# Attention's two heads of a pair in two corners of TensorE's array, with one copy each for queries and x

## The chip, the cores and the metric

The kernel runs on one core of one Trainium2 chip. A core has five engines with queues of their own: TensorE (PE; its weight loads are shown apart, as PEld), VectorE (DVE), ScalarE (ACT), GpSimd (POOL) and SyncE (SP), which issues most of the DMAs. Products are made by TensorE into PSUM; the other engines work on SBUF and PSUM. The metric is the device time of one execution in microseconds, as the median of several. Before the change it is 1930.49 us (three runs, 1930.45 to 1933.51).

## What is computed

Three stages follow each other, all on 2304 tokens of 512 numbers. The change lies in the first.

```python
scores = scale * np.matmul(q, k.transpose(0, 1, 3, 2))   # 4 batches, 8 heads, 576 positions, 64 numbers
mask = (rel >= 0) & (rel < window)                       # window = 64
attn = np.exp(scores - np.max(scores)) / sum
x = attn @ v                                             # 2304 x 512

P = exp(x @ w_gate), normed over rows and columns 8 times
x = sum over 8 experts of P[:, e] * (relu(x @ w1[e]) @ w2[e])

out = one expert per token, chosen greedily up to a capacity, relu(x @ w1[e]) @ w2[e]
```

A position sees only itself and the 63 before it. So a block of 64 queries needs 128 keys: its own block and the one ahead of it.

## The kernel before

**Tiles of attention.** The 2304 positions make 18 tiles of 128 (NT). A tile holds two blocks of 64 queries (b = 0, 1) and eight heads, taken as four pairs (HP = 4). After a transpose the 128 partitions hold the two heads of a pair, 64 numbers each.

**Queries** (function attn, lines 533 to 546). Four transposes put a tile's queries into a PSUM tile of pool psb. Then ScalarE copies them into qbd, once for each head of the pair (line 541), into a matrix that is zero elsewhere: rows 0 to 63 of head 0 beside columns 0 to 63, rows 64 to 127 of head 1 beside columns 64 to 127. So one product over 128 rows gives both heads' scores and does not mix them. The zeros are written once at the start, on GpSimd.

**Keys** (keys_of). They are transposed in the same way and copied by VectorE into a ring of six tiles, kring (line 580).

**Scores** (scores). Per block and pair one product of 128 rows, 128 weight columns (qbd) and 128 keys. For b = 1 both key blocks lie in one tile (line 591); for b = 0 they lie in two, which one product reads with a stride (line 597); in each sixth tile, where the ring wraps, it takes two products of 64 keys (line 600). VectorE adds the mask and takes the maximum (line 605), ScalarE exponentiates (line 612).

**Values** (values). Line 621 transposes the probabilities, ScalarE copies them to pTs (line 626, in the space of hh and hl). Line 632 multiplies: 128 keys as rows, the values of both heads as 128 weight columns, the probabilities of both heads as 128 moving columns. Of the four quarters of the result two are used, head 0 with head 0 and head 1 with head 1. So x leaves PSUM in two parts of 64 partitions: each is rounded to fp16 by ScalarE into xh (line 643), and VectorE stores the rest into xl (line 645).

**What else runs.** Expert 0 of the second stage is worked at the same time: its first layer at line 773, its second at line 943, its weights' splitting at lines 345 and 347. Router logits follow each tile of x (lines 683 and 685). The value maximum of each tile is spread over the partitions by a transpose with one column (line 266) and a product with one row (line 271). From expert 1 on the first layer is line 865.

**What sets the order.** A planner (class Flow) puts all of this in one order, while the program is built. Every step is a generator that asks for an engine with a cost in microseconds (Rq: PE 0.88 for a score step, ACT 0.53 for a copy of queries); the planner keeps a time for each engine, honours what a step depends on and the buffers of the pools (psb has four), and takes the task of lowest rank among those that can start within 0.12. Attention's tiles have ranks from 20 on, expert 0's products 50: those fill TensorE when attention has nothing ready. The costs are part of the text, so another cost means another order on all engines.

Of the kernel before, what the change touches and what calls it, by code (L numbers as in the profile page):

```python
# [8 lines left out]
F32 = mybir.dt.float32  # L9
F16 = mybir.dt.float16  # L10
I32 = mybir.dt.int32
AF = mybir.ActivationFunctionType
OP = mybir.AluOpType
# [159 lines left out]
def body(ctx, tc, q, k, v, wg1, w11, w12, wg2, w21, w22, out):  # L173
    nc = tc.nc
    V, A, PE, G, SP = nc.vector, nc.scalar, nc.tensor, nc.gpsimd, nc.sync
# [8 lines left out]
    HP = H // 2  # L184
# [8 lines left out]
    pss = ExitStack()  # L193
    ps1 = ctx.enter_context(tc.tile_pool(name="ps1", bufs=2, space=PSUM))
    ps2 = ctx.enter_context(tc.tile_pool(name="ps2", bufs=2, space=PSUM))
    psb = pss.enter_context(tc.tile_pool(name="psb", bufs=4, space=PSUM))
# [9 lines left out]
    xh = base.tile([128, DC, N], F16, name="xh")  # L206
    xl = base.tile([128, DC, N], F16, name="xl")
# [21 lines left out]
    abase = att.enter_context(tc.tile_pool(name="abase", bufs=1))  # L229
# [245 lines left out]

    qbd = []
    for i in range(2):
        t = abase.tile([128, 2, HP, 128], F32, name=f"qbd{i}")
        G.memset(t, 0.0)
        qbd.append(t)  # L480
    pTs = [t.rearrange("p a b -> p (a b)")[:, o:o + 1024].bitcast(F32).rearrange("p (h k) -> p h k", h=HP)
           for o in (0, 1024) for t in hbuf[1]]
    ldqk, ldv, ldvs = {}, {}, {}
# [1 line left out]
    KR = 6  # L485
    KT = HP * 128
    kring = abase.tile([128, (KR + 1) * KT], F32, name="kring")

    def kslot(i):
        o = (KR - 1 - i % KR) * KT  # L490
        return kring[:, o:o + KT].rearrange("p (h b q) -> p h b q", h=HP, b=2)
# [16 lines left out]
    def load_v(i):  # L508
        ldv[i] = apool.tile([128, H, D], F32, name="ldv", bufs=3)
        rows(ldv[i], v, i * 128, 128)  # L510
        fl.at["v", i] = fl.load(256)
# [17 lines left out]
    def attn(i):  # L529
        r = 20 + i if i else 0.5  # L530
        fl.add(keys_of(i), r)
        a = yield Rq("PE", 0.45, [("q", i), ("go", i - 2) if i > 1 else None], "psb")
        pq = psb.tile([128, HP, 128], F32, name="pb")
        t = ldqk.pop(("q", i)).rearrange("p h d -> p (h d)")
        for hp in range(HP):
            PE.transpose(pq[:, hp], t[:, hp * 128:(hp + 1) * 128], ident)
        qb = qbd[i % 2]
        for h2 in range(2):
            c = yield Rq("ACT", 0.53, [a.end])
            s = slice(h2 * 64, h2 * 64 + 64)  # L540
            A.activation(qb[s, :, :, s].rearrange("p b h q -> p h b q"),
                         pq[s].rearrange("p h (b q) -> p h b q", b=2), AF.Copy)
        fl.release("psb", a.idx, c.end)
        first = yield Rq("DVE", 0.01, [c.end, ("kT", i)], "pn")
        pn = apool.tile([128, 2, HP, 128], F32, name="pn")
        mx = small.tile([128, 8], F32, name="mx")
        nm = small.tile([128, 8], F32, name="nm")
        sm = small.tile([128, 8], F32, name="sm")
        for b in range(2):
            fl.add(scores(i, b, pn, mx, nm, sm), r)  # L550

        y = yield Rq("DVE", 0.5, [("ex", i, 0), ("ex", i, 1), ("vm", i), ("vm", max(i - 1, 0))])
        V.tensor_scalar(xinv[:, i:i + 1], vmax[:, i:i + 1], vmax[:, max(i - 1, 0):max(i - 1, 0) + 1], 1e-30,
                        op0=OP.max, op1=OP.max)
        V.tensor_scalar(sm, sm, 1e-9, xinv[:, i:i + 1], op0=OP.add, op1=OP.mult)
        rs = small.tile([128, 8], F32, name="rs")
        V.reciprocal(rs, sm)
        rc["pnleft", i] = 2
        for b in range(2):
            x = yield Rq("DVE", 0.66, [y.end])  # L560
            V.tensor_tensor(pn[:, b], pn[:, b], rs[:, b * HP:(b + 1) * HP, None].to_broadcast([128, HP, 128]), OP.mult)
            fl.add(values(i, b, pn, first.idx, x.end), r)

    def keys_of(i):
        b = yield Rq("PE", 0.45, [("k", i), ("go", i - 2) if i > 1 else None], "psb")
        pk = psb.tile([128, HP, 128], F32, name="pb")
        t = ldqk.pop(("k", i)).rearrange("p h d -> p (h d)")
        for hp in range(HP):
            PE.transpose(pk[:, hp], t[:, hp * 128:(hp + 1) * 128], ident)
        if i + 2 < NT:  # L570
            load_qk(i + 2)
        if i == 0:
            load_v(2)
            start_load(w2src(0), w2raw, 4, "w2r")
            SP.dma_start(wg2s, wg2.rearrange("(c p) e -> p c e", p=128))
            fl.at["wg2s"] = fl.load(16) + 8.0
        d = yield Rq("DVE", 0.66, [b.end])
        if i == 0:
            G.memset(kslot(-1)[:, :, 1], 0.0)
        V.tensor_copy(kslot(i), pk.rearrange("p h (b q) -> p h b q", b=2))  # L580
        fl.release("psb", b.idx, d.end)
        fl.at["kT", i] = d.end
        fl.add(largest_v(i), 5 + i)

    def scores(i, b, pn, mx, nm, sm):
        qb, kT = qbd[i % 2], kslot(i)
        f = yield Rq("PE", 0.88, [], "psb")
        pss = psb.tile([128, HP, 128], F32, name="pb")
        for hp in range(HP):
            if b:  # L590
                PE.matmul(pss[:, hp], qb[:, b, hp], kT[:, hp], start=True, stop=True)
            else:
                if i % KR:
                    o = (KR - 1 - i % KR) * KT + hp * 128
                    w = KT + 64
                    kk = kring[:, o:o + 2 * w].rearrange("p (b q) -> p b q", b=2)[:, :, 0:64]
                    PE.matmul(pss[:, hp].rearrange("p (b q) -> p b q", b=2), qb[:, b, hp], kk, start=True, stop=True)
                    continue
                for x, kk in enumerate((kT[:, hp, 0], kslot(i - 1)[:, hp, 1])):
                    PE.matmul(pss[:, hp, x * 64:x * 64 + 64], qb[:, b, hp], kk, start=True, stop=True)  # L600
        g = yield Rq("DVE", 1.0, [f.end])
        mk = masks[:, 2 * b + (1 if (2 * i + b) % NBLK == 0 else 0)]
        for hp in range(HP):
            u = b * HP + hp
            V.tensor_tensor_reduce(pn[:, b, hp], pss[:, hp], mk, 1.0, -3.0e38, OP.add, OP.max, mx[:, u:u + 1])  # L605
        us = slice(b * HP, b * HP + HP)
        V.tensor_scalar(nm[:, us], mx[:, us], -0.125, None, op0=OP.mult)
        fl.release("psb", f.idx, g.end)
        x = yield Rq("ACT", 1.55, [g.end])
        for hp in range(HP):  # L610
            u = b * HP + hp
            A.activation(pn[:, b, hp], pn[:, b, hp], AF.Exp, bias=nm[:, u:u + 1], scale=0.125, accum_out=sm[:, u:u + 1])
        fl.at["ex", i, b] = x.end
        if b:
            fl.at["go", i] = x.start

    def values(i, b, pn, held, dep):
        m = yield Rq("PE", 0.45, [dep], "psb")
        pp = psb.tile([128, HP, 128], F32, name="pb")
        for hp in range(HP):  # L620
            PE.transpose(pp[:, hp], pn[:, b, hp], ident)
        rc["pnleft", i] -= 1
        if not rc["pnleft", i]:
            fl.release("pn", held, m.end)
        n = yield Rq("ACT", 0.6, [m.end, ("av", 2 * i + b - 4) if i > 1 else None])
        A.activation(pTs[(2 * i + b) % 4], pp, AF.Copy, scale=8.0)
        fl.release("psb", m.idx, n.end)
        o = yield Rq("PE", 0.9, [n.end, ("vs", i)], "psb")
        vt = (ldvs[i], ldv[i])[b].rearrange("p h d -> p (h d)")
        px = psb.tile([128, HP, 128], F32, name="pb")  # L630
        for hp in range(HP):
            PE.matmul(px[:, hp], vt[:, hp * 128:(hp + 1) * 128], pTs[(2 * i + b) % 4][:, hp], start=True, stop=True)  # L632
        fl.at["av", 2 * i + b] = o.end
        if ("av", 2 * i + 1 - b) in fl.at:
            if i + 3 < NT:
                load_v(i + 3)
            if i + 2 < NT:
                load_vs(i + 2)
        c0 = i * 128 + b * 64
        for h2 in range(2):  # L640
            s = slice(h2 * 64, h2 * 64 + 64)
            x = yield Rq("ACT", 0.34, [o.end])
            A.activation(xh[s, :, c0:c0 + 64], px[s, :, s], AF.Copy)
            y = yield Rq("DVE", 0.4, [x.end])
            V.tensor_tensor(xl[s, :, c0:c0 + 64], px[s, :, s], xh[s, :, c0:c0 + 64], OP.subtract)  # L645
        fl.release("psb", o.idx, y.end)
        fl.at["xp", i, b] = y.end
        if ("xp", i, 1 - b) in fl.at:
            bg.done.add(("x", i))
            fl.at["x", i] = max(y.end, fl.at["xp", i, 1 - b])  # L650
# [739 lines left out]
    for e in range(1, E):  # L1390
        jobs += [(1, e), (0, e)]
        for _ in range(M2PLAN.get(e, len(m2left))):
            m, x = m2left.pop(0)
# [197 lines left out]
```

## Time and profile before

| | |
|---|---|
| median of three runs | 1930.49 us |
| profiled execution | 1943.79 us, span 1942.0 us |
| TensorE busy | 1859.8 us (96%) |
| VectorE busy | 1261.4 us (65%) |
| ScalarE busy | 916.1 us (47%) |
| mean granted clock of TensorE | 0.988 |

The profiled execution is some 13 us longer than the median; durations are read from it and compared with its own time. Products are pipelined: the next starts before the last has ended, so the pace of a burst is read from start to start and not from the mean duration. Attention ends at about 236 us, and the change concerns nothing behind it. A step at TensorE costs time at once if TensorE has work waiting; a step on another engine costs time only where TensorE waits for it.

### The profile page before, as it was taken

How to read it: one execution, taken by the hardware profiler on the slowest of the kernel's cores; microseconds unless marked ns; L12 is line 12 of the kernel's file. 1: busy time of each engine (PE TensorE's matmuls, PEld its weight loads, DVE VectorE, ACT ScalarE, POOL GpSimd, SP SyncE). 2: the span in 40 equal slices, each digit the busy share in tenths (PEclk: the TensorE clock that was granted, in tenths of full speed). 3: DMA queues.
4: the chain of work that ended last, by engine and by line, in shares of the span. 5: the costliest groups of instructions: out<-in, count | busy, mean ns of one | idle time of the engine just before them, and what ended most of it. 6: DMA issues, size and time to landing. Idle time of an engine off the chain costs nothing.

```text
span 1942.0 us, 39658 instructions
## 1 busy us (share of the span) xinstructions
PE 1859.8 (96%) x15605; PEld 1339.3 (69%) x15605; DVE 1261.4 (65%) x3845; ACT 916.1 (47%) x2493; POOL 110.8 (6%) x142
## 2 busy tenths in 40 slices
PE   6899999999999999999999999999999997899987
PEld 5777755776686766767766867677686773676765
DVE  7877796464666676676667666766747777465540
ACT  6777634552455555554554555455534442222222
POOL 0000000000000000000000000000000113223231
PEclk9999999999999999999999999999999998899999
DMA  8465301140134323323442434234231101435451
GB/s 188 89 131 120 83 1 44 59 160 1 55 120 143 119 93 118 138 88 116 145 136 83 131 117 145 93 99 157 88 104 28 43 20 64 175 123 172 159 211 29
DMA packets 172795, 203.32 MB, mean 105 GB/s; under 512 B 83000, under 2 KB 130104, under 8 KB 168512
## 3 DMA queue, kind: packets, MB, share of 16 engines
q1 hardware_dynamic: 164928, 157.78, 27.4%
q0 software_dynamic: 7680, 43.02, 6.3%
q8 instruction: 122, 2.00, 0.4%
q14 instruction: 65, 0.53, 0.1%
HBM read 143.05 MB, written 57.71 MB: 103 GB/s over the span
## 4 chain that ended last, share of the span: by engine, by line
PE 71%; DVE 11%; issue 6%; DMA 5%; ACT 4%; POOL 2%; SPq 0%; POOLq 0%; ACTq 0%; DVEq 0%
PE p L943 28%; PE p L865 17%; PE pb L865 12%; PE p L1302 4%; PE p L773 3%; DMA w2scr<-st2k 2%; DVE st2k L347 1%; DMA raw<-xrows,idx 1%; PE pb L1152 1%; DVE xl L645 1%; PE p L1314 1%; DMA raw<-in_moe_w_dram 1%; DMA ws<-st2k 1%; PE pb L632 1%; DVE pn L605 1%
## 5 line engine op out<-in xcount | busy, mean ns | idle before, releaser
L943 PE MATMUL p<-w2b,hh 128*128 128x512 f16 x2304 | 686.0, 379 | 0.0
L943 PE MATMUL p<-w2b,hl 128*128 128x512 f16 x1152 | 436.6, 379 | 0.0
L943 PEld LDWEIGHTS <-hh 128*128 128x128 f16 x2304 | 222.1, 99 | 218.2 <-issue 0.2
L865 PEld LDWEIGHTS <-w1b 128*128 128x128 f16 x4032 | 340.3, 98 | 22.2 <-issue 4.0
L865 PEld LDWEIGHTS <-w1x 128*128 128x128 f16 x3024 | 256.3, 98 | 21.1 <-issue 7.4
L865 PE MATMUL p<-th,w1x 128*128 128x192 f16 x1344 | 221.2, 246 | 4.3 <-ACT sa L877 2.2
L865 PE MATMUL pb<-xh,w1b 128*128 128x192 f16 x1344 | 221.3, 246 | 0.0
L943 PEld LDWEIGHTS <-hl 128*128 128x128 f16 x1152 | 112.6, 98 | 135.5 <-issue 0.6
L865 PE MATMUL pb<-xl,w1b 128*128 128x192 f16 x672 | 165.3, 246 | 0.0
L865 PE MATMUL p<-tl,w1x 128*128 128x192 f16 x672 | 165.3, 246 | 0.0
L347 DVE SCALAR_TENSOR_TENSOR st2k<-raw,wsc,st2k 128x512 f16<-128x512 f32 x128 | 91.9, 748 | 51.8 <-ACT st2k L345 51.5
L345 ACT ACTIVATE st2k<-raw,wsc 128x512 f16<-128x512 f32 x128 | 86.5, 713 | 71.3 <-DMA ws<-st2k 58.8
L959 DVE SCALAR_TENSOR_TENSOR acc<-p,SE,acc 128x512 f32<-128x512 f32 x126 | 94.0, 746 | 38.2 <-PE p L943 37.8
L1008 POOL TENSOR_TENSOR st2k<-tmp,st2k 128x512 f16<-128x512 f32 x18 | 24.7, 1370 | 1592.2 <-ACT tmp L1006 1571.1
L746 ACT ACTIVATE hh<-sb 128x192 f16<-128x192 f32 x168 | 61.0, 363 | 111.8 <-DVE sb L909 111.8
L865 PE MATMUL p<-th,w1b 128*128 128x192 f16 x672 | 110.6, 246 | 2.9 <-ACT sc L898 2.9
L746 ACT ACTIVATE hh<-sa 128x192 f16<-128x192 f32 x168 | 60.9, 363 | 107.2 <-DVE sa L883 107.2
L865 PE MATMUL pb<-xh,w1x 128*128 128x192 f16 x672 | 110.6, 246 | 0.0
L865 PE MATMUL p<-xh,w1b 128*128 128x192 f16 x672 | 110.6, 246 | 0.0
L883 DVE TENSOR_TENSOR sa<-pb,sa 128x192 f32<-128x192 f32 x168 | 60.0, 357 | 75.1 <-PE pb L865 72.6
L747 DVE SCALAR_TENSOR_TENSOR hl<-sa,hh 128x192 f16<-128x192 f32 x168 | 60.3, 359 | 72.1 <-ACT hh L746 72.1
L747 DVE SCALAR_TENSOR_TENSOR hl<-sb,hh 128x192 f16<-128x192 f32 x168 | 60.3, 359 | 71.7 <-ACT hh L746 71.7
(309 smaller groups left out, 3381.3 us busy)
## 6 DMA issues: line engine op xcount, KB each, us to landing
raw<-in_moe_w_dram SPq DMA_DIRECT2D x128, 512.0 KB, 5.6
ws<-st2k SPq DMA_DIRECT2D x128, 256.0 KB, 4.5
w2b<-w2scr SPq DMA_DIRECT2D x28, 512.0 KB, 7.1
w2scr<-st2k SPq DMA_DIRECT2D x48, 256.0 KB, 4.5
xrows<-st2k SPq DMA_DIRECT2D x18, 257.0 KB, 3.3
vs<-in_v_dram SPq DMA_DIRECT2D x35, 128.0 KB, 4.1
ldq<-in_q_dram SPq DMA_DIRECT2D x16, 256.0 KB, 4.6
ldk<-in_k_dram SPq DMA_DIRECT2D x16, 256.0 KB, 4.8
```

Source lines behind the costliest of these rows:

```text
L345: A.activation(hi, src, AF.Copy, scale=sc)
L347: V.scalar_tensor_tensor(lo, src, sc, hi, op0=OP.mult, op1=OP.subtract)
L605: V.tensor_tensor_reduce(pn[:, b, hp], pss[:, hp], mk, 1.0, -3.0e38, OP.add, OP.max, mx[:, u:u + 1])
L746: A.activation(hh[:, f, cols], src, AF.Relu)
L747: V.scalar_tensor_tensor(hl[:, f, cols], src, 0.0, hh[:, f, cols], op0=OP.max, op1=OP.subtract)
L773: PE.matmul(p[:, 0:w], w1v[wi][:, c, fs], x[:, c, ts], start=(n == 0), stop=(n == 3 * DC - 1))
L865: PE.matmul(bank[:, 0:HB], aq[wi][:, c, fs], xq[xi][:, c], start=(start and n == 0), stop=(n == 5), skip_group_check=True)
L883: V.tensor_tensor(t, b3[:, 0:HB], t, OP.add)
L943: PE.matmul(p, h[:, f, js], w2v[wi][:, f], start=(n == 0), stop=(n == 3 * FC - 1))
L959: V.scalar_tensor_tensor(acc[:, i], p, SE[:, e, i:i + 1], acc[:, i], op0=OP.mult, op1=OP.add)
L1008: G.tensor_tensor(xr[:, DM:2 * DM], xs, xr[:, 0:DM], OP.subtract)
L1302: PE.matmul(p[:, 0:CAP], wv1[f // 4][w][:, c, fs], xt[:, x * DC + c], start=(n == 0), stop=(n == 3 * DC - 1))
```

## The change

Queries are copied once, all 128 partitions, into a dense tile qT without zeros. The scores of the two heads of a pair become two products: head 0 with rows 0 to 63 and outputs 0 to 63, head 1 with rows 64 to 127 and outputs 64 to 127, so in two opposite corners of the array. The values become two products per pair as well: 64 weight columns and 64 moving columns each, head 0 to outputs 0 to 63, head 1 to outputs 64 to 127. The result is dense on 128 partitions, and x is copied once per block instead of twice. The planner's costs of the copies are set anew; those of the products stay.

```diff
--- before.py
+++ after.py
@@ -475,9 +475,7 @@
 
     qbd = []
     for i in range(2):
-        t = abase.tile([128, 2, HP, 128], F32, name=f"qbd{i}")
-        G.memset(t, 0.0)
-        qbd.append(t)
+        qbd.append(abase.tile([128, HP, 128], F32, name=f"qT{i}"))
     pTs = [t.rearrange("p a b -> p (a b)")[:, o:o + 1024].bitcast(F32).rearrange("p (h k) -> p h k", h=HP)
            for o in (0, 1024) for t in hbuf[1]]
     ldqk, ldv, ldvs = {}, {}, {}
@@ -534,12 +532,8 @@
         t = ldqk.pop(("q", i)).rearrange("p h d -> p (h d)")
         for hp in range(HP):
             PE.transpose(pq[:, hp], t[:, hp * 128:(hp + 1) * 128], ident)
-        qb = qbd[i % 2]
-        for h2 in range(2):
-            c = yield Rq("ACT", 0.53, [a.end])
-            s = slice(h2 * 64, h2 * 64 + 64)
-            A.activation(qb[s, :, :, s].rearrange("p b h q -> p h b q"),
-                         pq[s].rearrange("p h (b q) -> p h b q", b=2), AF.Copy)
+        c = yield Rq("ACT", 0.61, [a.end])
+        A.activation(qbd[i % 2], pq, AF.Copy)
         fl.release("psb", a.idx, c.end)
         first = yield Rq("DVE", 0.01, [c.end, ("kT", i)], "pn")
         pn = apool.tile([128, 2, HP, 128], F32, name="pn")
@@ -586,18 +580,20 @@
         qb, kT = qbd[i % 2], kslot(i)
         f = yield Rq("PE", 0.88, [], "psb")
         pss = psb.tile([128, HP, 128], F32, name="pb")
+
         for hp in range(HP):
-            if b:
-                PE.matmul(pss[:, hp], qb[:, b, hp], kT[:, hp], start=True, stop=True)
-            else:
-                if i % KR:
-                    o = (KR - 1 - i % KR) * KT + hp * 128
+            for s in (slice(0, 64), slice(64, 128)):
+                qs, o = qb[s, hp, b * 64:b * 64 + 64], pss[s, hp]
+                if b:
+                    PE.matmul(o, qs, kT[s, hp].rearrange("p b q -> p (b q)"), start=True, stop=True)
+                elif i % KR:
+                    c = (KR - 1 - i % KR) * KT + hp * 128
                     w = KT + 64
-                    kk = kring[:, o:o + 2 * w].rearrange("p (b q) -> p b q", b=2)[:, :, 0:64]
-                    PE.matmul(pss[:, hp].rearrange("p (b q) -> p b q", b=2), qb[:, b, hp], kk, start=True, stop=True)
-                    continue
-                for x, kk in enumerate((kT[:, hp, 0], kslot(i - 1)[:, hp, 1])):
-                    PE.matmul(pss[:, hp, x * 64:x * 64 + 64], qb[:, b, hp], kk, start=True, stop=True)
+                    kk = kring[s, c:c + 2 * w].rearrange("p (b q) -> p b q", b=2)[:, :, 0:64]
+                    PE.matmul(o.rearrange("p (b q) -> p b q", b=2), qs, kk, start=True, stop=True)
+                else:
+                    for x, kk in enumerate((kT[s, hp, 0], kslot(i - 1)[s, hp, 1])):
+                        PE.matmul(o[:, x * 64:x * 64 + 64], qs, kk, start=True, stop=True)
         g = yield Rq("DVE", 1.0, [f.end])
         mk = masks[:, 2 * b + (1 if (2 * i + b) % NBLK == 0 else 0)]
         for hp in range(HP):
@@ -627,9 +623,12 @@
         fl.release("psb", m.idx, n.end)
         o = yield Rq("PE", 0.9, [n.end, ("vs", i)], "psb")
         vt = (ldvs[i], ldv[i])[b].rearrange("p h d -> p (h d)")
-        px = psb.tile([128, HP, 128], F32, name="pb")
+        px = psb.tile([128, HP, 128], F32, name="pb")[:, :, 0:64]
         for hp in range(HP):
-            PE.matmul(px[:, hp], vt[:, hp * 128:(hp + 1) * 128], pTs[(2 * i + b) % 4][:, hp], start=True, stop=True)
+            for h2 in range(2):
+                s = slice(h2 * 64, h2 * 64 + 64)
+                PE.matmul(px[s, hp], vt[:, hp * 128 + h2 * 64:hp * 128 + h2 * 64 + 64], pTs[(2 * i + b) % 4][:, hp, s],
+                          start=True, stop=True)
         fl.at["av", 2 * i + b] = o.end
         if ("av", 2 * i + 1 - b) in fl.at:
             if i + 3 < NT:
@@ -637,12 +636,10 @@
             if i + 2 < NT:
                 load_vs(i + 2)
         c0 = i * 128 + b * 64
-        for h2 in range(2):
-            s = slice(h2 * 64, h2 * 64 + 64)
-            x = yield Rq("ACT", 0.34, [o.end])
-            A.activation(xh[s, :, c0:c0 + 64], px[s, :, s], AF.Copy)
-            y = yield Rq("DVE", 0.4, [x.end])
-            V.tensor_tensor(xl[s, :, c0:c0 + 64], px[s, :, s], xh[s, :, c0:c0 + 64], OP.subtract)
+        x = yield Rq("ACT", 0.36, [o.end])
+        A.activation(xh[:, :, c0:c0 + 64], px, AF.Copy)
+        y = yield Rq("DVE", 0.42, [x.end])
+        V.tensor_tensor(xl[:, :, c0:c0 + 64], px, xh[:, :, c0:c0 + 64], OP.subtract)
         fl.release("psb", o.idx, y.end)
         fl.at["xp", i, b] = y.end
         if ("xp", i, 1 - b) in fl.at:
```

TensorE, in the middle of attention: a run of value products followed by the scores of a tile and the transposes of the next tile's queries and keys. Each row gives the line, the result from its moving operand and weights, and weight columns by moving columns as the program writes them. Before:

```order
L632 MATMUL pb<-hh_81,vs 128x128 x4
L271 MATMUL pb<-mxr,ones 128x1
L621 MATMUL pb<-ident,pn 128x128 x12
L632 MATMUL pb<-hl_82,ldv 128x128 x4
L632 MATMUL pb<-hh_81,vs 128x128 x4
L632 MATMUL pb<-hl_82,ldv 128x128 x4
L597 MATMUL pb<-kring,qbd_128 128x128 x4
L591 MATMUL pb<-kring,qbd_128 128x128 x4
L536 MATMUL pb<-ident,ldq 128x128 x4
L569 MATMUL pb<-ident,ldk 128x128 x4
```

Now, in the corresponding place of the changed program:

```order
L617 MATMUL pb<-ident,pn 128x128 x12
L630 MATMUL pb<-hl_82,ldv 64x64 x8
L630 MATMUL pb<-hh_81,vs 64x64 x8
L630 MATMUL pb<-hl_82,ldv 64x64 x8
L596 MATMUL pb<-kring,qT_126 64x64 x16
L588 MATMUL pb<-kring,qT_126 64x128 x8
L534 MATMUL pb<-ident,ldq 128x128 x4
L563 MATMUL pb<-ident,ldk 128x128 x4
```

Each value step has eight products of 64x64 in the place of four of 128x128, each score step eight or sixteen. The shape changes three times here, from 128x128 to the half columns, to the corners and back.

ScalarE, in the first third of attention: the copies of probabilities (hh, hl), of x (xh) and the exponentials (pn). Before:

```order
L626 ACTIVATE hh_81<-pb 128x512
L626 ACTIVATE hl_82<-pb 128x512
L643 ACTIVATE xh<-pb 64x4x64 x2
L612 ACTIVATE pn,sm<-pn,nm 128x128 x4
L643 ACTIVATE xh<-pb 64x4x64 x2
L612 ACTIVATE pn,sm<-pn,nm 128x128 x12
```

Now:

```order
L622 ACTIVATE hh_81<-pb 128x512
L622 ACTIVATE hl_82<-pb 128x512
L640 ACTIVATE xh<-pb 128x4x64
L608 ACTIVATE pn,sm<-pn,nm 128x128 x4
L640 ACTIVATE xh<-pb 128x4x64
L608 ACTIVATE pn,sm<-pn,nm 128x128 x8
```

The copies of x stand as one row of 128 partitions where two of 64 stood.

TensorE, at the last value product of the last tile, with expert 0's first layer (p) and the router's products (wgs) beside it. Before:

```order
L773 LDWEIGHTS w1b
L773 MATMUL p_3002<-xl,w1b 128x384
L773 LDWEIGHTS w1b
L773 MATMUL p_3002<-xh,w1b 128x384
L632 MATMUL pb<-hl_82,ldv 128x128 x4
L683 LDWEIGHTS xh
L683 MATMUL pb<-wgs,xh 128x16
```

Now:

```order
L682 LDWEIGHTS xl
L682 MATMUL pb<-wgs,xl 128x8
L682 LDWEIGHTS xl
L682 MATMUL pb<-wgs,xl 128x8
L630 MATMUL pb<-hh_81,vs 64x64 x8
L630 MATMUL pb<-hl_82,ldv 64x64 x8
L680 LDWEIGHTS xh
L680 MATMUL pb<-wgs,xh 128x16
```

The last value product follows directly on the other one of its tile and on router products. By this place 384 products of line 773 (line 770 now) and 114 of line 943 (now 940) have been issued, where it was 480 and 144: attention is planned to end earlier among them.

## Rows read from the trace of the kernel before

**Rows 1.** The page, busy time of each engine with its share of the span.
```profile
PE 1859.8 (96%) x15605; PEld 1339.3 (69%) x15605; DVE 1261.4 (65%) x3845; ACT 916.1 (47%) x2493; POOL 110.8 (6%) x142
```

**Rows 2.** Stages: length, busy us of PE, PEld, DVE, ACT, POOL, clock, DMA.
```profile
0.00:50.00 50.00, 33.71 (x248) 29.54 (x249) 37.63 (x148) 31.64 (x88) 3.06 (x9) 0.93 0.80 183
50.00:100.00 50.00, 44.70 (x463) 38.84 (x462) 40.26 (x161) 37.45 (x128) 0.00 (x0) 1.00 0.45 86
100.00:240.00 140.00, 134.59 (x1036) 101.31 (x1034) 107.11 (x426) 98.78 (x317) 0.00 (x0) 1.00 0.53 116
240.00:300.00 60.00, 58.88 (x317) 31.36 (x316) 55.80 (x149) 20.49 (x41) 0.00 (x0) 1.00 0.00 1
300.00:600.00 300.00, 297.82 (x2347) 206.41 (x2346) 174.98 (x442) 137.98 (x373) 0.00 (x0) 1.00 0.25 80
```

**Rows 3.** The chain that ended last, 0 to 240 us, shares by line.
```profile
by line: PE p L773 11.4%; DVE xl L645 8.4%; PE pb L632 7.7%; PE p L943 7.0%; DVE pn L605 6.7%; ACT xh L643 6.2%; ACT pn L612 6.0%; PE pb L621 5.0%; issue 4.0%; DVE pn L561 2.6%; DVE kring L580 2.3%; PE pb L600 2.2%; DVE vm L526 2.1%; DMA w2
```

**Rows 4.** Waits, 0 to 240 us: waiter, releaser, us in total, times, longest.
```profile
PEld pb L621 <- ACT qbd L541: 1.3, 2, 0.8
PEld L683 <- ACT xh L643: 1.3, 2, 0.9
```

**Rows 5.** Groups by form, 0 to 240 us: copies; busy us, mean ns.
```profile
L645 DVE TENSOR_TENSOR xl<-pb,xh 64x256 f16<-64x256 f32 x72 | 30.0, 421 | 23.9 <-ACT xh L643 22.9
...
L643 ACT ACTIVATE xh<-pb 64x256 f16<-64x256 f32 x72 | 26.8, 377 | 23.6 <-DVE xl L645 14.1 <-PE pb L632 8.7
...
L541 ACT ACTIVATE qbd<-pb 64x512 f32<-64x512 f32 x36 | 21.2, 589 | 2.3 <-PE pb L536 1.5
...
L626 ACT ACTIVATE hh<-pb 128x512 f32<-128x512 f32 x18 | 10.7, 594 | 6.2 <-PE pb L621 6.1
```

**Rows 6.** Groups by form, 0 to 240 us: products; count, busy us, mean ns.
```profile
L632 PE MATMUL pb<-hh,vs 128*128 128x128 f32 x144 | 20.6, 290 | 0.5 <-ACT hl L626 0.3 <-ACT hh L626 0.2
...
L591 PE MATMUL pb<-kring,qbd 128*128 128x128 f32 x144 | 20.2, 286 | 0.0
...
L597 PE MATMUL pb<-kring,qbd 128*128 128x128 f32 x120 | 16.2, 278 | 0.0
...
L600 PE MATMUL pb<-kring,qbd 128*128 128x64 f32 x48 | 7.4, 322 | 0.0
```

**Rows 7.** Timeline of PE: start us, us to the last end, passes x count.
```profile
149.11 1.06 PE L597 MATMUL pb<-kring,qbd 128*128 128x128 f32 x8
150.01 1.06 PE L591 MATMUL pb<-kring,qbd 128*128 128x128 f32 x8
```

**Rows 8.** Timeline of PE, the scores in two pieces.
```profile
163.18 1.90 PE L600 MATMUL pb<-kring,qbd 128*128 128x64 f32 x16
164.91 0.33 PE L591 MATMUL pb<-kring,qbd 128*128 128x128 f32 x1
```

**Rows 9.** Timeline of PE, a transpose with one column.
```profile
110.46 0.27 PE L266 MATMUL pb<-ident,vm 128*1 128x128 f32 x1
110.57 0.59 PE L943 MATMUL p<-w2b,hh 128*128 128x512 f16 x2
```

**Rows 10.** Timeline of PE, the one-row product of line 271.
```profile
157.21 0.33 PE L773 MATMUL p<-xh,w1b 128*128 128x384 f16 x1
157.46 0.38 PE L271 MATMUL pb<-mxr,ones 1*128 1x1 f32 x2
157.77 0.66 PE L536 MATMUL pb<-ident,ldq 128*128 128x128 f32 x4
```

**Rows 11.** Timeline of PE, the product with 40 weight columns.
```profile
1618.18 0.59 PE L943 MATMUL p<-w2b,hh 128*128 128x512 f16 x2
1618.61 0.38 PE L943 MATMUL p<-w2b,hl 128*128 128x512 f16 x1
1618.92 0.61 PE L1152 MATMUL pb<-A,G 128*40 128x8 f16 x18
1619.46 0.60 PE L943 MATMUL p<-w2b,hh 128*128 128x512 f16 x2
```


## The prediction

> **What bounds the kernel now.** I read the page's busy times first: TensorE is busy for 96% of the span [rows 1], so whatever the other engines save can only arrive through the time in which TensorE waits. The stage table comes next [rows 2]. Attention lies between 0 and 240 us, among expert 0's products, which fill TensorE whenever attention has nothing ready. There TensorE is busy 33.71, 44.70 and 134.59 us of 50, 50 and 140, so it idles 16.3 + 5.3 + 5.4 = 27.0 us, four fifths of it in the first 100 us; VectorE (77% over the 240) and ScalarE (70%) are well filled too. From 300 to 600 us TensorE idles 2.2 us of 300. So two things are worth time: TensorE's own work in attention, and those 27 us. The third view is the chain of waits over 0 to 240 us [rows 3]: it runs for 8.4% and 6.2% (20.2 and 14.9 us) through the copies of x, which the change halves. Last, the waits view says how seldom TensorE itself names a copy that is cut: 1.3 us on xh, 1.3 on qbd [rows 4].
>
> **The copies (ScalarE, VectorE).** A copy of queries on 64 partitions with 512 elements takes 589 ns; a copy of the same 512 elements on 128 partitions takes 594 [rows 5]. So the number of partitions costs nothing, and one copy in the place of two saves a whole one. Queries: 18 tiles x 0.59 = 10.6 us of ScalarE. x: 36 x 0.377 = 13.6 us of ScalarE and 36 x 0.421 = 15.2 us of VectorE [rows 5]. None of this is on TensorE. Its worth lies between nothing below and the half of the chain's 35.1 us, 17.5 us, above. It can also be negative: the planner, which is told of shorter copies, now ends attention behind less of expert 0's work (384 layer-1 and 114 layer-2 products ahead of the last value product, where 480 and 144 were), so there is less to fill waits with. I take 5 us, nearer to the low end, since the waits on the cut copies are 2.6 us [rows 4], with 17.5 gained and 6 lost as ends. The two zero-fills that go stand on GpSimd, busy 3 us in the first 50 [rows 2]; I cost them at nothing.
>
> **The products (TensorE).** In fp32 every product is two passes (the counts in [rows 6] are twice the products). How long is a pass? Eight follow each other in 0.90 us, from 149.11 to 150.01: 0.111 each [rows 7]. With half the moving columns (64), 16 take 1.73 us: still 0.108 [rows 8]. So there the weights set the pace, 128 columns of fp32 in 0.11. And the one-column transpose at 110.46 holds back the next product by 0.11 with 128 moving columns and almost no weights [rows 9]. So a pass costs the larger of two terms that both are 0.11 at 128 columns; I estimate half, 0.056, at 64 columns.
>
> Now the products one by one. All have twice as many passes after the change, in two corners.
> - Values: 288 passes now (144 in the row, as many with the other half of the tiles, ldv), 288 x 0.111 = 32.0 us. Then 576, with 64 weight columns and 64 moving. If the corners run side by side, 288 x 0.056 = 16.1 us: 15.9 saved. One after the other, 576 x 0.056 = 32.3: nothing saved. If 64 columns cost as much as 128 and nothing overlaps, 63.9: 31.9 lost.
> - Scores with 128 keys (144 + 120 passes): 264 x 0.111 = 29.3 us. Then 528 passes with 64 weight columns, but still 128 moving: side by side 29.3 (no change), one after the other 58.6 (29.3 lost).
> - Scores in two pieces (48 passes): 5.3 us; side by side 48 x 0.056 = 2.7 (2.6 saved), in turn no change.
> Whether two corners overlap, no row shows, since no product of this kernel uses any place but the first. What speaks for it is that the two corners share neither rows nor columns of weights or outputs, and that a weight load already runs beside the product ahead of it (1339 us of load within 1860 of product [rows 1]). I take side by side.
> The Trainium skill, "TensorE: Matmul & The Clock Gate", Part 3 on row and column tiling, says that products in distinct strips start within some 4 ns of each other, and gives speedups of 2.4 to 3.1 for three and four of them. No run here shows it; by it the sum is the one I take.
>
> **The changes of shape.** Here the trace has a price. The one-row product at line 271 starts 0.25 us (157.21 to 157.46) after a pass of 384 columns, which takes 0.16 at the pace of 0.215 for 512 [rows 11], and its two passes hold up the next transpose 0.31 us where 2 x 0.11 would do [rows 10]: 0.09 in, 0.09 out. The product of 40 weight columns at line 1152 starts 0.31 us after a pass of 0.215, and its 18 passes of 0.025 take 0.54 to the next: again 0.09 and 0.09 [rows 11]. The transpose with one column at 110.46 paid nothing [rows 9], so not every narrow shape does. Counting in the new order, score products stand in 26 stretches and value products in 27, some back to back; that makes 76 changes of shape beyond those at line 271. 76 x 0.09 = 6.9 us lost; bounds 0 and, if each lost a whole fp32 pass more, 76 x 0.20 = 15.
>
> **Sum.** TensorE: -15.9 - 2.6 + 0 + 6.9 = -11.6 us. Up to 100 us TensorE waits for others for a fifth of the time, and shorter work there becomes longer waiting; some 40% of the tiles lie there. I let a third of the saving go: -7.7. With 5 for the copies: -12.7 us. The profiled execution took 1943.8 us (span 1942.0), 13.3 above the median of 1930.5; taken off, 1931.1 there and **1918 us** as median. Behind attention TensorE's order holds the same instructions, from expert 1 on nearly all in the same places, so I move nothing there.
>
> **Rivals.**
> 1. The weights don't overlap. Products run side by side, but the corners' weights come in one after the other, 2 x 0.056 for a pair. Then scores and values cost what they did, and only the changes of shape (6.9) and the copies (-5) are left: 1932, from 1925 to 1940. For it: the 64-column scores were paced by their weights alone [rows 8]. Against: weights of separate corners need not share a path.
> 2. The scores' two corners don't overlap, because both write the same PSUM tile pb at once. Scores +29.3, values -15.9, changes +6.9: TensorE +20.3, of which a fifth falls into waits that exist, +16; copies -5; 1941. It decides as soon as the score burst after is near 1.8 us where it was 0.90. The trace has no two writers in one tile to judge by.
> The Trainium skill, "TensorEngine Tiling (Array Packing)", Restrictions and Gotchas, says that different row tiles cannot access the same PSUM bank at the same time; that rule would make it so. No run here shows it so far.
> 3. Nothing overlaps: passes of both corners in turn. Scores +29.3, values +0.3, changes +6.9 = +36.5, a fifth hidden: +29; copies -5; 1954, and more if 64 columns cost what 128 do. Slower; place: lines 588 to 630 on TensorE; it decides once a pair of passes takes over some 0.15 us. For it: all passes of the trace start one after the other. Against: nothing in it was ever given two places.
> 4. The saving of TensorE is real, but attention is paced by ScalarE and VectorE, whose passes over scores (masks, exponentials, transposes' copies) are untouched: TensorE waits instead, and the time stays, 1927 to 1933.
>
> **How the numbers follow.** Forecast 0.40; rival 1 0.20; rival 2 0.15; rival 3 0.17; rival 4 0.08. The forecast's own range is 1908 to 1926: 17.5 or -6 for the copies, 0 to 15 for the changes of shape, not all at one end. Up to 1950, it takes in rivals 1, 2 and 4 and the low edge of rival 3; what lies above, down to the outer bounds of the passes, is left out with a little below 1908. A measurement can tell 0.2%, 3.9 us. Faster by more: nearly all of the forecast, a fifth of rival 1, a quarter of rival 4: 0.43. Within: half of rival 1, most of rival 4: 0.17. Slower: rivals 2 and 3, the rest of 1: 0.40.
>
> **What would show it.** A value burst of 16 passes in about 0.45 us shows the overlap, 0.9 rival 1 or 3. A score burst of 0.9 us shows the corners side by side, 1.8 rival 2 or 3. The first pass of a burst 0.09 us late shows the change of shape. The copies must take 0.59, 0.38 and 0.42 us at half the count. TensorE's idle time of 0 to 240 us shows the rest: near 25 us if the copies gave 5 and a third of the saving went into waits; above 35 it is rival 4. The prediction fails if passes in the corners cost something other than a share of 0.11, or if the end moves by what happens behind 300 us.

## The result, and the profile after

The changed kernel takes 1916.47 us (median of 4 runs, 1912.47 to 1918.16), beside 1931.01 for the kernel before (4 runs): ratio 0.9906, 95% interval 0.9887 to 0.9925. On another chip the pair gave 0.9896 (0.9880 to 0.9913). The forecast was 1918 us with a range of 1908 to 1950, and faster by more than 0.2% with the largest chance; it is faster by more.

The kernel before takes 1931 to 1946 us on the chips that were used, so experiments are compared by their ratio to it, and by a mark in the trace that lies ahead of the last stage: the start of expert 1's first product, behind which TensorE's order is nearly that of before. In two profiled executions of the changed kernel, on two chips, it stood at 330.04 and 330.3 us. The clock granted to TensorE does move this mark, as is shown below. Before:

```profile
347.88 0.25 PE L865 MATMUL p<-xh,w1b 128*128 128x192 f16 x1
```
After:

```profile
330.04 0.25 PE L862 MATMUL p<-xh,w1b 128*128 128x192 f16 x1
```
So 17.8 us are gained up to there, and the distance keeps to 18 us up to the last pass of the last expert's first layer (it starts at 1598.1 and 1579.9). The two profiled spans differ by 27.6; the rest arises in the last stage, where both do the same work. The profiled execution of before was 13 us above its median, so I do not count that rest.

The page's busy line after, for [rows 1]:

```profile
PE 1845.1 (96%) x16205; PEld 1319.9 (69%) x16205; DVE 1242.6 (65%) x3808; ACT 889.8 (46%) x2439; POOL 107.7 (6%) x140
```
The stages, up to expert 1's start (columns as in [rows 2]):

```profile
0.00:50.00 50.00, 32.62 (x343) 27.42 (x343) 39.17 (x156) 31.05 (x94) 1.27 (x7) 0.86 0.85 183
50.00:100.00 50.00, 47.85 (x711) 40.42 (x711) 37.67 (x174) 32.33 (x123) 0.00 (x0) 0.97 0.50 108
100.00:240.00 140.00, 138.89 (x1392) 93.00 (x1389) 114.62 (x456) 78.32 (x266) 0.00 (x0) 1.00 0.36 78
240.00:330.00 90.00, 87.46 (x470) 45.99 (x470) 55.97 (x108) 39.62 (x79) 0.00 (x0) 1.00 0.21 71
```
TensorE is busy 306.8 of 330 us, where it was 319.8 of 347.9: 13.0 us less busy time and 4.9 us less idle time (28.1 to 23.2). Most of the idle time that is left lies in the first 50 us (17.4); from 50 to 240 us it fell from 10.7 to 3.3. The last value product stands at 193.8 us (234.6 before), with less of expert 0's work ahead of it.

The clock column differs as well: 0.86 and 0.97 in the first two stages, where it was 0.93 and 1.00 [rows 2]. The granted clock has two levels in these traces, 2.4 GHz (1.00) and 1.2 GHz (0.50). Up to expert 1 TensorE is busy for 14.4 us at the lower one, where it was 6.6. What that costs is seen in a value step at 0.50:

```profile
46.79 1.12 PE L630 MATMUL pb<-hh,vs 128*64 128x64 f32 x16
47.84 0.58 PE L271 MATMUL pb<-mxr,ones 1*128 1x1 f32 x2
```
It takes 1.05 us to the next product; the same sixteen passes at 1.00 take 0.62 (123.41, below). By these two steps I estimate that 0.41 of the busy time at 1.2 GHz is lost: some 6 us now and some 3 before. At one clock, TensorE's busy time would then have fallen by some 16 us and not by 13. No run here shows why the clock falls in one order of the program and not in another.

The chain of 0 to 240 us, for [rows 3], no longer names a copy of x among its larger pieces:

```profile
by line: PE p L770 16.3%; PE p L940 10.6%; PE pb L630 9.2%; PE pb L617 7.1%; PE pb L588 5.4%; PE pb L593 5.2%; DVE pn L601 3.5%; ACT pn L608 2.6%; DVE pn L555 2.5%; PE pb L563 2.3%; PE pb L271 2.2%; DMA vs<-in_v_dram 2.1%; PE pb L534 2.1%; 
```
The copies by form, for [rows 5]: half as many, each as long as one was. (Here and below, three dots stand for rows left out.)

```profile
L642 DVE TENSOR_TENSOR xl<-pb,xh 128x256 f16<-128x256 f32 x36 | 14.9, 419 | 15.0 <-ACT xh L640 14.8
L640 ACT ACTIVATE xh<-pb 128x256 f16<-128x256 f32 x36 | 13.5, 380 | 9.2 <-PE pb L630 8.7
...
L536 ACT ACTIVATE qT<-pb 128x512 f32<-128x512 f32 x18 | 10.3, 586 | 5.3 <-PE pb L534 5.2
```
TensorE's bursts, for [rows 7, 8]. First a value step, ahead of a transpose; then two score steps in a row behind a value step; then scores in two pieces:

```profile
123.41 0.69 PE L630 MATMUL pb<-hh,vs 128*64 128x64 f32 x16
124.03 0.27 PE L266 MATMUL pb<-ident,vm 128*1 128x128 f32 x1
...
112.02 1.09 PE L593 MATMUL pb<-kring,qT 64*64 64x128 f32 x16
112.95 1.04 PE L588 MATMUL pb<-kring,qT 64*64 64x128 f32 x16
113.92 0.55 PE L563 MATMUL pb<-ident,ldk 128*128 128x128 f32 x3
...
140.35 1.20 PE L596 MATMUL pb<-kring,qT 64*64 64x64 f32 x32
141.33 1.09 PE L588 MATMUL pb<-kring,qT 64*64 64x128 f32 x16
```
Eight value passes before, with the next scores behind them:

```profile
165.86 1.06 PE L632 MATMUL pb<-hl,ldv 128*128 128x128 f32 x8
166.75 1.06 PE L597 MATMUL pb<-kring,qbd 128*128 128x128 f32 x8
```
Sixteen passes of values take 0.62 us to the next product, where eight took 0.89. Sixteen of scores take 0.93 with the first pair's extra, where eight took 0.90. Thirty-two small ones take 0.98, where sixteen took 1.73. In the trace's own times the passes stand in pairs: the two corners start 6 to 7 ns apart (13 to 14 in the scores in two pieces), and the next pair starts 58 ns (64 moving columns) or 109 ns (128) after the last. The corners do run side by side, with weights and all.

### The profile page after: what moved, and what is told of

It is laid out like the page before. It is cut to its first block, busy times and chain, and to the rows that moved or that the text cites. A ratio compares the mean times of both kernels' runs of the same rounds, so it can differ in the third digit from the quotient of the medians.

```text
span 1914.4 us, 40759 instructions
## 1 busy us (share of the span) xinstructions
PE 1845.1 (96%) x16205; PEld 1319.9 (69%) x16205; DVE 1242.6 (65%) x3808; ACT 889.8 (46%) x2439; POOL 107.7 (6%) x140
## 4 chain that ended last, share of the span: by engine, by line
PE 74%; DVE 9%; DMA 7%; issue 5%; ACT 3%; POOL 1%; SPq 0%; POOLq 0%; ACTq 0%; DVEq 0%
PE p L940 27%; PE p L862 17%; PE pb L862 12%; PE p L770 4%; PE p L1299 4%; DMA ws<-st2k 2%; DMA raw<-in_moe_w_dram 2%; DVE st2k L347 1%; DMA raw<-xrows,idx 1%; PE pb L630 1%; DMA w2scr<-st2k 1%; PE pb L1149 1%; PE p L1311 1%; ACT st2k L345 1%; PE pb L617 1%
## 5 line engine op out<-in xcount | busy, mean ns | idle before, releaser
L862 PEld LDWEIGHTS <-w1b 128*128 128x128 f16 x4032 | 340.3, 98 | 22.9 <-issue 4.2
L295 ACT ACTIVATE st2k<-raw 128x512 f16<-128x512 f32 x116 | 72.3, 624 | 80.4 <-DMA raw<-in_moe_w_dram 52.0
```

The costliest lines, as they stand in the source:

```text
L295: A.activation(junk[:, 0:512], s0, AF.Square, accum_out=mp[:, c:c + 1])
L862: PE.matmul(bank[:, 0:HB], aq[wi][:, c, fs], xq[xi][:, c], start=(start and n == 0), stop=(n == 5), skip_group_check=True)
```

## The experiments

| kernel | ratio to before, 95% interval | expert 1 starts, us | TensorE idle up to there, us | of its busy time, at 1.2 GHz |
|---|---|---|---|---|
| before | 1 | 347.9 | 28.1 | 6.6 |
| changed | 0.9906 (0.9887-0.9925) | 330.0 | 23.2 | 14.4 |
| changed, again | 0.9896 (0.9880-0.9913) | 330.3 | 23.0 | 15.2 |
| values in turn | 0.9952 (0.9933-0.9970) | 340.2 | 22.9 | 18.2 |
| scores in turn | 0.9981 (0.9969-0.9994) | 345.2 | 22.0 | 8.9 |
| two copies | 0.9959 (0.9947-0.9971) | 340.6 | 32.0 | 9.9 |
| two copies, order of one | 0.9978 (0.9963-0.9993) | 347.3 | 33.3 | 14.7 |
| values only | 0.9907 (0.9890-0.9924) | 334.5 | 26.7 | 10.5 |
| scores only | 0.9967 (0.9953-0.9981) | 348.1 | 28.4 | 9.0 |
| measured costs | 0.9882 (0.9868-0.9896) | 330.8 | 23.0 | 18.4 |
| extra product ahead | 0.9929 (0.9910-0.9949) | 341.1 | 23.0 | 17.0 |
| extra product between | 0.9970 (0.9956-0.9983) | 349.3 | 20.6 | 23.8 |
| in turn, parted | 1.0048 (1.0027-1.0068) | 362.8 | 23.1 | 14.1 |
| fewer changes of shape | 0.9873 (0.9852-0.9895) | 326.5 | 24.9 | 0.0 |

Each mark is from one profiled execution. It does not say all: the ratio of "scores only" is below 1 while its mark is not. The last column is TensorE's busy time at the lower clock up to the mark, in us. By the estimate above 0.41 of it is lost, so where two rows differ by 5 us in it, some 2 us between their marks are the clock's. The cuts of the programs below show changed lines alone.

**Values in turn.**
```diff
-        for hp in range(HP):
-            for h2 in range(2):
+        for h2 in range(2):
+            for hp in range(HP):
```


> Values: the four products of head 0 first, then the four of head 1, so that neighbours stand in the same half of the columns and cannot run side by side. Same work, copies and order of steps. Theory (the gain of TensorE is the overlap of the two halves): 16 passes take 16 x 0.058 in the place of 8 pairs x 0.058, +0.47 us in each of 36 value steps, +16.7 us of TensorE; between two thirds and all of it arrives: 1927 to 1933 us. Rival (weights set the pace, or the copies alone brought the gain): a step of 16 passes takes what it took, 1916 us.

Expert 1 started 10.2 us later, not 16.7: value passes grew by 9.0 us, 0.25 a step. The starts of one step's 16 passes show why (us):

```
111.617 .724 .782 .840 | .899 .904 .957 112.011 .015 .069 .074 .128 | .186 .244 .303 .361
```
Four passes go alone, then come close pairs, then four alone again. The pass at 111.904 takes 270 ns like the first of a half (the others 222). So the first pass of head 1, which the program has in the ninth place, started beside the fifth of head 0: passes of a free half start ahead of waiting ones of a busy half. The theory holds in its direction, and all of the 9 us arrived (some 1.5 of the 10.2 are the clock's, by the estimate).

**Scores in turn.**
```diff
-        for hp in range(HP):
-            for s in (slice(0, 64), slice(64, 128)):
+        for s in (slice(0, 64), slice(64, 128)):
+            for hp in range(HP):
```

> Scores: head 0 of the four pairs first, then head 1, so that neighbours stand in the same corner. Theory (two corners side by side, though they write one PSUM tile): 16 passes x 0.109 in the place of 8 pairs x 0.109, +0.87 us in each of 33 score steps and some +0.9 in three, +31 us of TensorE; two thirds to all arrive: 1937 to 1948 us. Rival (both corners write one PSUM tile and are already served in turn): 1916 us.

```profile
98.55 1.58 PE L593 MATMUL pb<-kring,qT 64*64 64x128 f32 x16
100.06 0.60 PE L940 MATMUL p<-w2b,hh 128*128 128x512 f16 x2
```
A step takes 1.51 us where it took 1.02 alone. Score passes grew by 15.9 us, about half of 31, the starts showing the same overtaking; expert 1 started 15.2 us later, with some 2 us less lost to the clock. The rival is out: two corners writing one PSUM tile are not served in turn.

**In turn, parted**, with its two controls, **extra product ahead** and **between**. The extra product (here as placed between the heads):
```diff
+            if h2:
+                PE.matmul(pz[:, 0, 64:128], ident, ident[:, 0:64], start=True, stop=True)
```


> The changed kernel with one extra product of full width (128 rows, 128 columns, 64 moving, two passes; its result is used nowhere) ahead of the eight products of each value step. 36 x 0.22 = 8.0 us of passes, and by the order 137 changes of shape in attention where the changed kernel has 114: 23 x 0.092 = 2.1 us. Theory (TensorE's time arrives in full, and a change of shape costs 0.09 us): expert 1 starts at 340 us in the place of 330. Rival (a third of what TensorE does there falls into waits, as forecast): 337.

> The same extra product, but in the middle of each value step, between the products of the second and the third pair: 186 changes of shape in the place of 137, the same passes. Theory (0.09 us a change, and 0.05 for the first pair behind it): 49 x 0.092 + some 36 x 0.05 = 6.3 us later than with the product ahead, expert 1 at 346 us. Rival (a change of shape is hidden where products stand back to back): within 1.5 us of the run with the product ahead.

> The same extra product in the middle of each value step, and ahead of it the four products of head 0, behind it the four of head 1: the same passes and changes of shape as with pairs on either side, but nothing that could run side by side. Without the extra product, in-turn values lost 0.25 us a step and not 0.47: their trace shows four passes alone, four pairs, four alone. Theory (TensorE lets passes of the other half overtake four that wait, and a change of shape in between forbids it): 8 x 0.058 = 0.47 us more a step than with pairs on either side, expert 1 16 to 17 us later than there. Rival (in-turn passes are simply paced at less than 0.058): 9 us later.

A value step with the extra product between pairs:

```profile
117.17 0.38 PE L943 MATMUL p<-w2b,hl 128*128 128x512 f16 x1
117.48 0.45 PE L633 MATMUL pb<-hh,vs 128*64 128x64 f32 x8
117.86 0.43 PE L630 MATMUL pb<-ident 128*128 128x64 f32 x2
118.22 0.45 PE L633 MATMUL pb<-hh,vs 128*64 128x64 f32 x8
118.61 0.98 PE L617 MATMUL pb<-ident,pn 128*128 128x128 f32 x7
```
The same with the heads parted by it:

```profile
121.49 0.38 PE L943 MATMUL p<-w2b,hl 128*128 128x512 f16 x1
121.80 0.68 PE L633 MATMUL pb<-hh,vs 128*64 128x64 f32 x8
122.41 0.43 PE L630 MATMUL pb<-ident 128*128 128x64 f32 x2
122.77 0.68 PE L633 MATMUL pb<-hh,vs 128*64 128x64 f32 x8
123.38 0.87 PE L617 MATMUL pb<-ident,pn 128*128 128x128 f32 x6
```
Ahead: 11.1 us later (10.1 expected in full, 7 if a third were hidden); some 1 us of it is the clock's by the estimate. Between: another 8.2 (6.3 expected, 1.5 by the rival), of which some 3 are the clock's. So a change of shape has its price, and TensorE's time arrives nearly in full. Parted: eight passes take 0.61 us where four pairs take 0.38, and expert 1 starts 13.5 us later still, against 16 to 17 and 9 expected; the value passes themselves grew by 15.5. Here the clock gave back some 4 us, and with them the 13.5 come to 17.5. Without a chance to overtake, nearly all of the overlap is gone; the kernel, with the extra product in it, is slower than before the change. Beside the run with the product between pairs, this is the worth of the values' overlap, measured by itself.

**Two copies**, and **two copies in the order of one.**
```diff
-        c = yield Rq("ACT", 0.61, [a.end])
-        A.activation(qbd[i % 2], pq, AF.Copy)
+        for h2 in range(2):
+            c = yield Rq("ACT", 0.53, [a.end])
+            s = slice(h2 * 64, h2 * 64 + 64)
+            A.activation(qbd[i % 2][s], pq[s], AF.Copy)
```
and so for xh and xl.

> The products of the changed kernel, but queries and x copied in two parts of 64 partitions each as before, with the planner's old costs for them. Theory (the copies are worth about 5 us): 1921 us. Rival A (they are worth half of the chain that runs through them, 17.5 us): 1934 us. Rival B (ScalarE and VectorE are nowhere the bound): 1916 us.

> Two copies of 64 partitions each, as in the run with two copies, but all instructions in the order of the changed kernel (the planner is told the costs of one copy). In the first such run TensorE's idle time ahead of expert 1 rose from 23.2 to 32.0 us and the ratio was 0.005 above the whole change. Theory (it is the time that the copies take): the same again, +0.004 to +0.006 over the changed kernel, idle time 30 us or more. Rival (it is the planner's other order, which the old costs bring): no more than +0.001.

Two copies cost 10.6 us at expert 1's start with a planner that knows of them, and 17.3 with one that does not. The idle time rose to 32.0 and 33.3 us: the time of the copies it is, not the order. Some of the loss is saved when the planner is told: the two runs are 6.7 us apart, of which some 2 are the clock's. TensorE's part from 50 to 100 us in the first of the two:

```profile
50.00:100.00 50.00, 42.90 (x631) 35.06 (x629) 39.82 (x160) 38.63 (x131) 0.00 (x0) 1.00 0.44 91
```
It idles 7.1 us there, where the changed kernel idles 2.2.

**Values only**, and **scores only.** Each takes one half of the change and puts the other back, here the products of values only:
```diff
-                qs, o = qb[s, hp, b * 64:b * 64 + 64], pss[s, hp]
-                    PE.matmul(o, qs, kT[s, hp].rearrange("p b q -> p (b q)"), start=True, stop=True)
+                PE.matmul(pss[:, hp], qb[:, b, hp], kT[:, hp], start=True, stop=True)
```
and of scores only:
```diff
-                PE.matmul(px[s, hp], vt[:, hp * 128 + h2 * 64:hp * 128 + h2 * 64 + 64], pTs[(2 * i + b) % 4][:, hp, s],
-                          start=True, stop=True)
+            PE.matmul(px[:, hp], vt[:, hp * 128:(hp + 1) * 128], pTs[(2 * i + b) % 4][:, hp], start=True, stop=True)
```

> The changed values (two column halves, one copy of x), but queries and scores as in the kernel before (block-diagonal qbd, two copies). Theory (values give all of TensorE's gain: passes from 34.8 to 22.5 us by the two traces, less some 2.5 for changes of shape; scores give nothing and pay some 3 for their own changes of shape): as fast as the whole change or 1 to 3 us faster, 1913 to 1917 us. Rival (the gain is the shorter chain of copies, queries and x alike): half of it, 1922 to 1924 us.

> The changed queries and scores (corners, one copy of queries), but values and x as before. Theory (the corners of the scores save TensorE some 1 us of passes and pay some 2.5 for 26 changes of shape; one copy less of queries gives 1 to 3): ratio to the kernel before 0.998 to 1.000. Rival (the corners are where the gain is): 0.994 or less.

Values only: 13.3 of the 17.8 us at expert 1's start, and a ratio like that of the whole change. Scores only: nothing at that mark, though its ratio (0.9967) says some 6 us for the whole execution; where those would come from I have not found. Behind 1600 us its mean granted clock was 0.96, beside 0.94 in the profiled execution of before, so the last stage may have a part in it; no run here sets that apart. The parts do not add up to the whole at the mark (13.3 - 0.2 and 17.8); that a dense copy of queries is worth more once TensorE's values are short is argued, not shown.

**Measured costs**, and **fewer changes of shape.** The first sets the two PE costs, 0.88 for a score step and 0.9 for a value step, to 1.1 and 0.7; the second:
```diff
-        x = self.free[r.eng]
+        x = self.free[r.eng] + (0.2 if r.eng == "PE" and r.shape != self.shape else 0.0)
-            x, t = min(((x, t) for x, t in c if x <= lo + 0.12), key=lambda v: (v[1][1], v[0]))
+            x, t = min(((x, t) for x, t in c if x <= lo + 0.22), key=lambda v: (v[1][1], v[0]))
-        f = yield Rq("PE", 0.88, [], "psb")
+        f = yield Rq("PE", 0.92, [], "psb", shape=1)
-        o = yield Rq("PE", 0.9, [n.end, ("vs", i)], "psb")
+        o = yield Rq("PE", 0.52, [n.end, ("vs", i)], "psb", shape=2)
```


> The changed kernel with the planner told what the steps take by the trace after: 1.1 us for a score step (0.88 before) and 0.7 for a value step (0.9). Same instructions, another order. Theory (the planner's picture of TensorE was wrong by up to 0.2 us a step, and its waits come from that): TensorE's idle time ahead of expert 1 falls by 3 us or more, -0.0015 to -0.003. Rival (errors of 0.2 us are lost among waits of the first 100 us): within 0.001 of the changed kernel.

> The changed kernel with a planner that knows TensorE's shape: a step in another shape than the last counts 0.2 us later, steps within 0.22 are taken by rank (0.12 before), and score and value steps are told as 0.92 and 0.52. Same instructions in another order, 86 changes of shape in the place of 114. Theory (28 x 0.092 = 2.6 us of TensorE, and TensorE's time arrives in full): expert 1 at 327 us, ratio to the kernel before 0.0013 below the changed kernel. Rival (steps that wait for their like make others late): no earlier than 330.

Costs alone brought nothing that can be told (330.8; its ratio's interval overlaps that of the changed kernel). Fewer changes brought expert 1 to 326.5 us, where 327 was expected, and the lowest ratio of all, whose interval overlaps the changed kernel's. The theory is not shown by that, since the clock differs. The first two stages of this run:

```profile
0.00:50.00 50.00, 33.29 (x400) 29.16 (x400) 37.42 (x154) 31.02 (x98) 1.27 (x7) 1.00 0.82 192
50.00:100.00 50.00, 45.66 (x676) 38.31 (x675) 40.16 (x177) 34.69 (x127) 0.00 (x0) 1.00 0.46 99
```
TensorE had 2.4 GHz all the way to expert 1, while the changed kernel lost some 6 us there by the estimate, more than the 3.5 that were gained. At 2.4 GHz a value pass takes 36 ns to the next product in the changed kernel, as a mean, and 37 here, so a saving on value steps does not show. The five executions of this run have a mean granted clock of 0.989 to 0.992, the ten of the changed kernel 0.985 to 0.990. The hit at 327 is therefore luck as far as this run can tell. Four value steps that now stand in a row:

```profile
123.64 0.69 PE L634 MATMUL pb<-hh,vs 128*64 128x64 f32 x16
124.16 0.64 PE L634 MATMUL pb<-hl,ldv 128*64 128x64 f32 x16
124.63 0.64 PE L634 MATMUL pb<-hh,vs 128*64 128x64 f32 x16
125.09 0.64 PE L634 MATMUL pb<-hl,ldv 128*64 128x64 f32 x16
```
With no change of shape between them, a step takes 0.465 us: eight pairs of 0.058.

## Why the prediction was right, point by point

- **The forecast's case** (corners side by side) is the one that came. Rivals 1 to 3 fall by the bursts: 0.62 us for values (0.465 where no change of shape stands between) and 0.93 for scores, not 0.9 and 1.8. Rival 4 falls because TensorE's idle time of 0 to 240 us did not grow: 20.6 us, where it was 27.0.
- **A pass is the larger of two terms, each half at 64 columns.** The estimate was 0.056; the trace has 0.058 a pair, and 0.109 for 128 moving columns.
- **Values -15.9, scores 0 and -2.6, changes of shape +6.9: -11.6.** TensorE's busy time up to expert 1 fell by 13.0 us, and by the estimate would have fallen by some 16 at one clock. From each value pass to the next product it is 34.8 us before and 22.5 after, for scores 38.5 and 37.4; the price of leaving a shape is in these sums. The price is 0.09 to enter and 0.09 to leave, as read from [rows 10, 11]. What I did not have is that the first pair behind a change takes 0.05 more (0.107 and 0.160 in the trace, in the place of 0.058 and 0.109).
- **A third of TensorE's saving goes into waits: +3.9.** With two copies it did: the idle time was 32.0 us with the new products, 28.1 with the old. With one copy it fell to 23.2, and five of the experiments show TensorE's time arriving nearly in full. So the step was wrong for the changed kernel; that it holds for a stage that the copies hold up rests on the one comparison.
- **The clock.** The forecast has no term for it, though [rows 2] showed 0.93 in the first 50 us. By the estimate it took some 3 us more from the changed kernel than from the one before.
- **The copies, 5 us of a range of -6 to 17.5.** This term was mis-sized: it measured 10.6 us by the run with two copies (some 2 more at one clock) and 17.3 with the order held fixed. I took the low end since TensorE's own waits named these copies for 2.6 us only [rows 4]. Where the 17.3 us were lost, TensorE's weight loads still named them for only 4.8 us. A late copy also delays a release of psb and the logits, and TensorE may then wait for another engine; that is my reading, and no run shows it by itself. The chain [rows 3] was the better guide here: half of its pieces on x is 17.5. That this is so near to 17.3 is partly chance, since the run also copies the queries twice.
- **The sum.** Forecast -12.7 us, of it -7.7 by TensorE and -5 by the copies; at expert 1's start -17.8, of it -13.0 in busy and -4.9 in idle time, within the forecast's own range. By the medians it is -14.5, which stands at the low edge of the ratio's interval (-14.5 to -21.8). That the median came within 2 us of 1918 is therefore partly luck.
- **The bank rule.** The Trainium skill, "TensorEngine Tiling (Array Packing)", Restrictions and Gotchas, would have made rival 2 come true. The trace disagrees for two diagonal corners that write different partitions of one PSUM tile: they start 7 ns apart. For two row tiles that write the same partitions no run here says anything.
- **Side by side.** The Trainium skill, "TensorE: Matmul & The Clock Gate", Part 3, has starts 4 ns apart in distinct strips; here they are 6 to 7, and 13 to 14 in the scores in two pieces.

## What to carry to other kernels

A product that fills its operands with zeros or throws away half its result can be cut into corners, if neighbours in TensorE's order stand in different corners; then two passes cost what one did, and with half the weight columns and half the moving columns less. A change of shape costs some 0.2 us in and out together, so steps of one shape in a row are worth a try; that an order with fewer changes is faster, no run here shows apart from the clock. Where a chain of waits runs through a copy, size the copy by the chain too, and not only by the waits that name it. Before a few us between two orders are put down to the order, compare the granted clock of the stage.

## What was not expected of the hardware

- TensorE starts passes out of the program's order where their half of the array is free: the ninth beside the fifth (values in turn), which saved about half of what in-turn order should have cost. An extra product of full width in between prevents it.
- The first pair behind a change of shape takes 0.05 us more than the next ones.
- Orders of the same instructions got different clocks up to expert 1: the changed kernel had TensorE busy at 1.2 GHz for 14.4 us, the order with fewer changes of shape for none.
